# A three-stage float32 kernel: conversion step, weight sums and state-unit loads put in another order

## The chip, the cores and the metric

One core of a Trainium2 chip runs the whole program. The metric is the device time of one execution in microseconds (us), as the median of several runs. All arithmetic is float32; a product is made of three matmuls on pairs of a high and a low part (a value rounded to the matmul's format, and the rest). What the tables call PE is the matmul engine (TensorE), DVE is VectorE, ACT is ScalarE, POOL is GpSimd, and SP is the engine whose queue issues every DMA here.

## The reference

```python
scores = scale * np.matmul(x, state.transpose(0, 1, 3, 2))      # B=8, H=8, S=512, Ns=32, D=64
a = softmax(scores); xread = np.matmul(a, state)
scores2 = scale * np.matmul(state, x.transpose(0, 1, 3, 2))
a2 = softmax(scores2); sread = np.matmul(a2, x)
x = concat([xread, sread]).transpose(0, 2, 1, 3).reshape(4352, 512)
gate = 1.0 / (1.0 + np.exp(-(x @ w_gate))); val = x @ w_val     # w_gate, w_val: 512 x 1536
x = (gate * val) @ w_out                                        # w_out: 1536 x 512
h = x @ w_in; e = np.exp(h - h.max(-1)); solu = h * e / e.sum(-1)   # w_in: 512 x 1024
ln = (solu - mean) / np.sqrt(var + 1e-6) * g_ln
out = ln @ w_out2                                               # w_out2: 1024 x 512
```

The weights arrive as float64. The kernel reads their 32-bit words and builds float32 from them.

## The kernel before

The first two stages go through nine blocks: seven batches, then all state reads together (the block SREAD, 256 tokens wide), then the last batch (in the code `last`, 512 tokens wide). Each block walks c = 0 to 11 over the twelve chunks of 128 hidden columns. In a chunk `first_mm` makes gate and value sums, `sigma` (ACT) and `gated` (DVE) make their product, `gated_hi` (ACT) and `gated_lo` (DVE) split it into `gh` and `gl`, and `out_acc(c-1)` adds the product of the chunk before to four banks `acc`. So the matmul engine works one chunk behind the gate.

For the batches the state is multiplied into the weights ahead of use: a "unit" of 128 x 512 is loaded from DRAM into one of four buffers `spill` (`state_load`, L566 for batches 4 to 7), and `state_w` splits it into `mh` (ACT) and `ml` (DVE). For batches 4 to 7 the units are made by `quad_w` (matmuls L605, copies L610 and L612 into `qst`, DMA L613 to `qsp`) in blocks 2 to 4 and come back from `qsp`, where a unit lies as four pieces of 32 rows.

During SREAD and `last` the weights of the third stage are converted: a `Conv` object loads a tile of words (`load`), takes it apart on ACT (`take`, two ACTIVATEs L207 and L208), forms the float on DVE (`form`, L215, L218, L224), adds the low bits on POOL (`add`, L234) and splits the float into high and low part (`split`). Two buffers hold words (`xn`), two hold floats (`tt`). `step(1)` does this for one tile in each chunk from c = 2. For `w_in` (in SREAD) the split is ACT L134 and POOL L243; for `w_out2` (in `last`) it multiplies by the layer-norm gain as well, ACT L245 (`woh`) and DVE L246 (`wol`). Eight tiles each: taken in c = 2 to 9, split one chunk later.

In `last`, `w_steps` are 24 small steps that make sums and differences of the `w_in` blocks (DVE L739, L742) and split them (ACT L134, DVE L747) into T1 to T4. A table says how many stand in each chunk. After the loop `put` splits the four `acc` banks, and the third stage begins: `h2_mm` for the first tile, its maximum (L788), exponentials, and so on. The first part of that stage is ordered by a scheduler; all before it stands in the order in which it is written, engine by engine, as does the rest of the third stage behind that part.

```python
        def step(self, n):
            for _ in range(len(self.joined)):
                self.split()
            m = min(n, len(self.loaded))
            for _ in range(m):
                self.take()
            self.form(m)
            for _ in range(m):
                self.add()
            for _ in range(n):
                self.load()
```

Of the kernel before, what the change touches and what calls it, by code (L numbers as in the profile page):

```python
# [28 lines left out]
def attn_moe_moe2_kernel(ctx: ExitStack, tc: tile.TileContext, x, state, w_gate, w_val, w_out, w_in2, w_out2, g_ln, out):  # L29
# [4 lines left out]
    nc = tc.nc  # L34
    B, H, S, D = x.shape
    NS = state.shape[2]
# [5 lines left out]
    KC = C // P  # L42
# [36 lines left out]
    spill = [x[:, 512 * i:512 * i + 512] for x in stg for i in range(2)]  # L79
# [42 lines left out]
    qsp = [tc.dram_tile([H, P, 512], F32, name=f"qsp{p}") for p in range(NF1 // 2)]  # L122
# [16 lines left out]
    def lo_of(dst, src, hi):  # L139
        return vec.tensor_tensor(out=dst, in0=src, in1=r(hi), op=ALU.subtract)  # L140
# [17 lines left out]
    class Conv:  # L158
# [87 lines left out]
                vec.scalar_tensor_tensor(out=l, in0=t, scalar=scale, in1=r(h), op0=ALU.mult, op1=ALU.subtract)  # L246

        def step(self, n):
            for _ in range(len(self.joined)):
                self.split()  # L250
            m = min(n, len(self.loaded))
            for _ in range(m):
                self.take()
            self.form(m)
            for _ in range(m):
                self.add()
            for _ in range(n):
                self.load()
# [266 lines left out]
    def ps_acc(m, n):  # L525
        return acc[m][:, 0:n]


    def put(src, h, l, hi=hi_of):
        return hi(h, src), lo_of(l, src, h)  # L530
# [28 lines left out]
    def state_load(b, n):  # L559
        if b < QUAD:  # L560
            nc.sync.dma_start(out=spill[n % 4], in_=msp[b][n])
            return
        p, g = divmod(n, 2)
        r0 = NS * (b - QUAD)
        for k in range(KC):
            nc.sync.dma_start(out=spill[n % 4][NS * k:NS * k + NS], in_=qsp[p][2 * k + g, r0:r0 + NS])  # L566

    def start8(b, p, o, to):

# [97 lines left out]
    def out_acc(c, n, ms=range(KC)):  # L667
        h, l = woh[c], wol[c]
        i = c % 2
        for m in ms:  # L670
            sl = slice(m * P, (m + 1) * P)
            mm3(ps_acc(m, n), h[:, sl], l[:, sl], gh[i][:, 0:n], gl[i][:, 0:n], c == 0, c == NF1 - 1)
# [24 lines left out]
    def yhl(q, k):  # L697
        return yh[q % 2][k], yl[q % 2][k]
# [94 lines left out]
    def h2_mm(i, f, k):  # L793
        q, b, t = tiles[i]
        h, l = yhl(q, k)
        w1, w2 = win(k, f)
        sl = slice(t * P, (t + 1) * P)
        mm3(h2_out(i, f), h[:, sl], l[:, sl], w1, w2, k == 0, k == KC - 1)
# [138 lines left out]
    def loads(n):  # L937

        nonlocal loaded
        loaded = max(loaded, made - M0)  # L940
        while loaded < min(made - M0 + n, len(ring)):
            b, p, g = ring[loaded]
            if b < PAIR and (b, p) in first8 or b < QUAD and early8 and early8[0] <= (b, p) or b >= QUAD and quads and quads[0] <= (p, KC - 1):
                return
            state_load(b, 2 * p + g)
            loaded += 1
# [14 lines left out]
    with tc.manual_schedule():  # L961
# [119 lines left out]
        c = NF1 - 3  # L1081
# [93 lines left out]
        for n_b, b in enumerate(blocks[1:], 1):  # L1175
            before = blocks[n_b - 1]
            n_before = S if before < B else SR
            n = S if b < B else SR
            last = n_b == len(blocks) - 1
            parts = attention(n_b + 1) if n_b + 1 < B else []  # L1180
            if last:
# [18 lines left out]
                w_steps = w_pair_ops([sbf.tile([P, 512], F32, name=f"bf{i}") for i in range(8)])  # L1200
# [5 lines left out]
            for c in range(NF1):  # L1206
# [72 lines left out]
                elif (b == SREAD or last) and c > 1:  # L1279
                    conv.step(1)  # L1280
                if last:
                    for _ in range((3, 3, 1, 2, 1, 2, 1, 2, 1, 2, 3, 2)[c]):
                        w_steps.pop(0)()
        act(stat[0][:, 0:1], half, AF.Exp)
        out_acc(NF1 - 1, S)
        w_steps.pop(0)()
        for k in range(KC):
            ends = put(ps_acc(k, S), *yhl(0, k))
        for k in range(KC):
            for f in range(2):  # L1290
                h2_mm(0, f, k)
# [38 lines left out]
    with tc.manual_schedule():  # L1330
        for i in range(len(first), nt, 2):
            q, b, t = tiles[i]
            n = 3 * ((S if b < B else SR) // P // 2)
# [25 lines left out]
            if i == len(first):  # L1359
                operand()  # L1360
            product(i, 3, w, False, True)
            next_ops(q, ops, step, n)
            plus(w, w, u2)
            h_max(i, 1)
# [71 lines left out]
```

## Time and profile before

| | before |
|---|---|
| median of 3 runs | 1076.2 us (1075.43 to 1076.49) |
| the profiled execution | 1077.1 us, span 1075.3 us |
| PE busy | 1049.0 us, 98% of the span |
| PE weight load busy | 826.8 us, 77% |
| DVE busy | 744.7 us, 69% |
| ACT busy | 569.5 us, 53% |
| POOL busy | 373.5 us, 35% |
| granted PE clock | 0.8 to 0.9 of full in the first slices of 27 us, 0.9 or more after |
| DMA | 148.30 MB, 44.0% of 16 engines on the queue that SP issues on |
| loads of quad state units (L566) | 192 DMAs of 64 KB |

Busy times are sums over the span. The span of the profile is a little shorter than the time of the execution that it belongs to, because starting and ending lie outside it. A row of a timeline gives start and duration of an instruction, its engine and line, the operation, output and inputs, and in brackets how long the engine was idle before it and what it waited for. Instructions of one engine overlap a little, so the distance of two starts can be shorter than the first one's duration.

### The profile page before, as it was taken

Reading aid. Unit: us, or ns where it says so; the run is one execution under the profiler, and the core shown is the slowest. Engines: PE = TensorE matmul, PEld = TensorE weight load, DVE = VectorE, ACT = ScalarE, POOL = GpSimd, SP = SyncE. Lnnn points to the kernel's source line nnn. Section 1 sums busy time; section 2 is a strip of 40 time slices with the busy share of each in tenths; the row PEclk is TensorE's granted clock in tenths of the full one; section 3 lists DMA queues with packets and bytes.
Section 4 is the critical chain, followed back from the end, with each engine's and each line's share of the span. In section 5 each row is a group of like instructions: output and inputs, shape, how many; then the busy total and the mean of one; then the engine's idle time right before and its main releaser. Section 6 shows DMA issues by size and latency. Waiting matters only on the chain.

```text
span 1075.3 us, 16622 instructions
## 1 busy us (share of the span) xinstructions
PE 1049.0 (98%) x5691; PEld 826.8 (77%) x5691; DVE 744.7 (69%) x1323; ACT 569.5 (53%) x1101; POOL 373.5 (35%) x429
## 2 busy tenths in 40 slices
PE   8889999999999999999999999999999999999998
PEld 5555667778877767878878988877888887888887
DVE  5898946658566456565574578968687778777773
ACT  5777645446435434434353455655656555655653
POOL 2687522124000000000000251343767757667551
PEclk8899999999999999999999999999999999999999
DMA  8964183451462662441521434304344444453441
GB/s 221 315 213 162 65 244 121 143 167 38 132 211 102 186 220 84 123 118 46 151 66 50 139 116 156 101 20 157 117 157 155 153 143 138 166 167 121 163 128 39
DMA packets 155740, 148.30 MB, mean 138 GB/s; under 512 B 74888, under 2 KB 115080, under 8 KB 155656
## 3 DMA queue, kind: packets, MB, share of 16 engines
q1 hardware_dynamic: 155656, 147.25, 44.0%
q8 instruction: 44, 0.72, 0.3%
q14 instruction: 40, 0.33, 0.1%
HBM read 91.10 MB, written 56.10 MB: 137 GB/s over the span
## 4 chain that ended last, share of the span: by engine, by line
PE 73%; DVE 9%; DMA 4%; issue 4%; POOL 4%; SPq 3%; ACT 3%; POOLq 0%; DVEq 0%; ACTq 0%
PE acc L143 10%; PE acc L144 9%; PE acc L145 9%; PE att L145 5%; PE att L143 5%; PE att L144 5%; PE gps L143 4%; PE gps L144 4%; PE gps L145 4%; PE vps L143 4%; PE vps L144 4%; PE vps L145 4%; POOL tt L234 1%; PE gps L605 1%; DMA usp<-ub 1%
## 5 line engine op out<-in xcount | busy, mean ns | idle before, releaser
L143 PE MATMUL acc<-gh,woh 128*128 128x512 f32 (+1 forms) x428 | 170.1, 398 | 0.9 <-ACT gh L134 0.9
L144 PE MATMUL acc<-gl,woh 128*128 128x512 f32 (+1 forms) x428 | 162.9, 381 | 1.9 <-DVE gl L665 1.9
L145 PE MATMUL acc<-gh,wol 128*128 128x512 f32 (+1 forms) x428 | 162.7, 380 | 0.0
L234 POOL TENSOR_TENSOR tt<-tt,xn 128x512 int32<-128x512 int32 x16 | 23.5, 1472 | 397.6 <-DVE tt L224 379.4
L659 DVE TENSOR_TENSOR sg<-vps,sg 128x512 f32<-128x512 f32 (+1 forms) x96 | 64.6, 672 | 133.9 <-PE vps L145 97.2
L655 ACT ACTIVATE sg<-gps 128x512 f32<-128x512 f32 (+1 forms) x96 | 55.8, 581 | 141.5 <-PE gps L145 139.3
L143 PEld LDWEIGHTS acc<-gh,woh 128*128 128x128 f32 x428 | 81.0, 189 | 41.1 <-issue 25.1
L134 ACT ACTIVATE gh<-sg 128x512 fp32r<-128x512 f32 (+1 forms) x102 | 61.5, 603 | 74.7 <-DVE sg L659 74.7
L144 PEld LDWEIGHTS acc<-gl,woh 128*128 128x128 f32 x428 | 81.1, 189 | 15.6 <-DVE gl L665 3.0
L145 PEld LDWEIGHTS acc<-gh,wol 128*128 128x128 f32 x428 | 80.9, 189 | 15.7
L870 POOL TENSOR_TENSOR wol<-ut,woh 128x512 fp32r<-128x512 f32 x48 | 61.6, 1299 | 89.7 <-ACT woh L134 87.7
L665 DVE TENSOR_TENSOR gl<-sg,gh 128x512 fp32r<-128x512 f32 (+1 forms) x96 | 66.9, 697 | 19.8 <-ACT gh L134 15.9
L145 PE MATMUL att<-woh,wol 128*128 128x512 f32 (+1 forms) x204 | 79.7, 390 | 0.7 <-POOL wol L870 0.6
L143 PE MATMUL att<-woh,woh 128*128 128x512 f32 (+1 forms) x204 | 79.8, 391 | 0.0
L144 PE MATMUL att<-wol,woh 128*128 128x512 f32 (+1 forms) x204 | 79.3, 389 | 0.0
L143 PE MATMUL gps<-ah,mh 128*128 128x512 f32 x178 | 70.9, 398 | 1.8 <-ACT qst L610 1.1
L144 PE MATMUL gps<-al,mh 128*128 128x512 f32 x178 | 70.1, 394 | 1.2 <-DVE al L140 1.2
L143 PE MATMUL vps<-ah,mh 128*128 128x512 f32 x178 | 69.6, 391 | 0.6 <-DVE ml L140 0.6
L145 PE MATMUL gps<-ah,ml 128*128 128x512 f32 x178 | 69.8, 392 | 0.0
L145 PE MATMUL vps<-ah,ml 128*128 128x512 f32 x178 | 69.4, 390 | 0.0
L144 PE MATMUL vps<-al,mh 128*128 128x512 f32 x178 | 69.3, 390 | 0.0
L544 POOL TENSOR_TENSOR xo<-wf,xe 128x512 fp32r<-128x512 f32 x24 | 32.6, 1364 | 96.6 <-ACT xe L134 91.5
(497 smaller groups left out, 2719.3 us busy)
## 6 DMA issues: line engine op xcount, KB each, us to landing
usp<-ub SPq DMA_DIRECT2D x32, 512.0 KB
ut<-usp SPq DMA_DIRECT2D x128, 128.0 KB
qsp<-qst SPq DMA_DIRECT2D x48, 256.0 KB
stg<-qsp SPq DMA_DIRECT2D x192, 64.0 KB
stg<-msp SPq DMA_DIRECT2D x36, 256.0 KB
out_dram<-sg SPq DMA_DIRECT2D x32, 256.0 KB
xn<-in_x_dram SPq DMA_DIRECT2D x15, 512.0 KB
msp<-pst SPq DMA_DIRECT2D x26, 256.0 KB
```

The source lines that it names most:

```text
L134: return act(dst, src, AF.Copy)
L143: mm(o, lh, rh, start=start, stop=False, **kw)
L144: mm(o, lh, rl, start=False, stop=False, **kw)
L145: return mm(o, ll, rh, start=False, stop=stop, **kw)
L234: pool.tensor_tensor(out=ti, in0=ti, in1=lo, op=ALU.add)
L544: pool.tensor_tensor(out=l, in0=w, in1=r(h), op=ALU.subtract)
L605: mm(o, s[h, k, :], w[h], start=n == 0, stop=n == 2)
L655: act(sg[c % 2][:, 0:n], gate_val(b, c)[0][:, 0:n], AF.Sigmoid)
L659: vec.tensor_tensor(out=g, in0=gate_val(b, c)[1][:, 0:n], in1=g, op=ALU.mult)
L665: eng.tensor_tensor(out=gl[c % 2][:, 0:n], in0=sg[c % 2][:, 0:n], in1=r(gh[c % 2][:, 0:n]), op=ALU.subtract)
L870: pool.tensor_tensor(out=lv, in0=wv[:, 4 * q:4 * q + 4], in1=r(hv), op=ALU.subtract)
```

## The change

Three edits. `step` takes the next tile apart before it splits the last one. The loop over four pieces in `state_load` becomes one DMA whose source is the four pieces as one pattern. The table of `w_steps` ends in 0, 0 in place of 3, 2, and the six steps that are left are issued behind the four `put`s, in the part that the scheduler orders.

```diff
         def step(self, n):
-            for _ in range(len(self.joined)):
-                self.split()
-            m = min(n, len(self.loaded))
+            m, done = min(n, len(self.loaded)), len(self.joined)
             for _ in range(m):
                 self.take()
+            for _ in range(done):
+                self.split()
             self.form(m)
@@ state_load
-        for k in range(KC):
-            nc.sync.dma_start(out=spill[n % 4][NS * k:NS * k + NS], in_=qsp[p][2 * k + g, r0:r0 + NS])
+        nc.sync.dma_start(out=spill[n % 4], in_=qsp[p].rearrange("(k g) r f -> g k r f", g=2)[g][:, r0:r0 + NS])
@@ last
                 if last:
-                    for _ in range((3, 3, 1, 2, 1, 2, 1, 2, 1, 2, 3, 2)[c]):
+                    for _ in range((3, 3, 1, 2, 1, 2, 1, 2, 1, 2, 0, 0)[c]):
                         w_steps.pop(0)()
         act(stat[0][:, 0:1], half, AF.Exp)
         out_acc(NF1 - 1, S)
-        w_steps.pop(0)()
         for k in range(KC):
             ends = put(ps_acc(k, S), *yhl(0, k))
+        for f in w_steps:
+            f()
```

On ACT in SREAD, one chunk. `gh` is the gate's high part, `xe` the high part of a `w_in` tile, `tt` and `xn` are the two results of a take. Before:

```order
L655 ACTIVATE sg_109<-gps 128x256
L134 ACTIVATE gh_95<-sg_109 128x256
L134 ACTIVATE xe_1209<-tt_104 128x512
L207 ACTIVATE tt_103<-xn_99 128x512
L208 ACTIVATE xn_99<-xn_99 128x512
```

The same chunk with the change:

```order
L654 ACTIVATE sg_109<-gps 128x256
L134 ACTIVATE gh_95<-sg_109 128x256
L207 ACTIVATE tt_103<-xn_99 128x512
L208 ACTIVATE xn_99<-xn_99 128x512
L134 ACTIVATE xe_1209<-tt_104 128x512
```

The high part of the last tile has moved behind both instructions of the take.

On ACT in `last`, chunk 4. Before:

```order
L134 ACTIVATE gh_95<-sg_109 128x512
L245 ACTIVATE woh_66<-tt_104,glnt 128x512
L207 ACTIVATE tt_103<-xn_99 128x512
L208 ACTIVATE xn_99<-xn_99 128x512
L134 ACTIVATE T2h_5441<-bf_5471 128x512
```

With the change:

```order
L134 ACTIVATE gh_95<-sg_109 128x512
L207 ACTIVATE tt_103<-xn_99 128x512
L208 ACTIVATE xn_99<-xn_99 128x512
L245 ACTIVATE woh_66<-tt_104,glnt 128x512
L134 ACTIVATE T2h_5315<-bf_5345 128x512
```

`woh` moved in the same way; on DVE the rows of this chunk (gl, `wol`, then L215, L218, L224) stand as they stood.

On DVE, from the gate of chunk 10 to the first maximum of the third stage. Before:

```order
L665 TENSOR_TENSOR gl_97<-sg_109,gh_95 128x512
L246 SCALAR_TENSOR_TENSOR wol_84<-tt_104,glnt,woh_72 128x512
L742 TENSOR_TENSOR bf_5475<-bf_5475,bf_5472 128x512
L747 TENSOR_TENSOR T3l_5448<-bf_5473,T3h_5447 128x512
L739 TENSOR_TENSOR bf_5474<-xe_1214,xo_1215 128x512
L659 TENSOR_TENSOR sg_110<-att_183,sg_110 128x512
L665 TENSOR_TENSOR gl_98<-sg_110,gh_96 128x512
L747 TENSOR_TENSOR T2l_5444<-bf_5475,T2h_5443 128x512
L742 TENSOR_TENSOR bf_5474<-bf_5474,bf_5475 128x512
L747 TENSOR_TENSOR T4l_5452<-bf_5474,T4h_5451 128x512
L140 TENSOR_TENSOR ml<-acc_176,mh 128x512
```

With the change (the lines are one lower behind the shorter `state_load`):

```order
L664 TENSOR_TENSOR gl_97<-sg_109,gh_95 128x512
L246 SCALAR_TENSOR_TENSOR wol_84<-tt_104,glnt,woh_72 128x512
L658 TENSOR_TENSOR sg_110<-att_183,sg_110 128x512
L664 TENSOR_TENSOR gl_98<-sg_110,gh_96 128x512
...
L140 TENSOR_TENSOR wol_85<-acc_179,woh_73 128x512
L741 TENSOR_TENSOR bf_5349<-bf_5349,bf_5346 128x512
L746 TENSOR_TENSOR T3l_5322<-bf_5347,T3h_5321 128x512
L738 TENSOR_TENSOR bf_5348<-xe_1214,xo_1215 128x512
L746 TENSOR_TENSOR T2l_5318<-bf_5349,T2h_5317 128x512
L741 TENSOR_TENSOR bf_5348<-bf_5348,bf_5349 128x512
L746 TENSOR_TENSOR T4l_5326<-bf_5348,T4h_5325 128x512
L787 TENSOR_REDUCE stat_125<-acc_176 128x1
```

Three operations left the place between the two gates, three more the place behind the second, and all six stand behind the four low parts of `put`.

## Rows read from the trace of the kernel before

**Rows 1.** Timeline, one turn of the conversion in SREAD (start us, us, engine, line)
```profile
611.01 1.30 POOL L234 TENSOR_TENSOR tt<-tt,xn 128x512 int32<-128x512 int32 x1 [1.61 <-issue]
...
612.35 0.63 ACT L134 ACTIVATE xe<-tt 128x512 fp32r<-128x512 f32 x1 [0.68 <-POOL tt L234]
...
615.96 1.31 POOL L234 TENSOR_TENSOR tt<-tt,xn 128x512 int32<-128x512 int32 x1 [1.61 <-issue]
```

**Rows 2.** Timeline of PE, start of one group of sums in SREAD
```profile
636.69 0.28 PE L143 MATMUL acc<-gh,woh 128*128 128x256 f32 x1
637.41 0.39 PE L144 MATMUL acc<-gl,woh 128*128 128x256 f32 x1 [0.43 <-DVE gl L665]
637.63 0.28 PE L145 MATMUL acc<-gh,wol 128*128 128x256 f32 x1
637.75 0.28 PE L143 MATMUL acc<-gh,woh 128*128 128x256 f32 x1
```

**Rows 3.** Busy us of PE, PEld, DVE, ACT, POOL (count); clock, DMA share, GB/s
```profile
666.00:703.30 37.30, 37.28 (x165) 30.57 (x164) 36.56 (x55) 22.66 (x40) 11.46 (x7) 1.00 0.35 101
```

**Rows 4.** Timelines of DVE and PE, last two gates of the last row
```profile
704.65 0.69 DVE L665 TENSOR_TENSOR gl<-sg,gh 128x512 fp32r<-128x512 f32 x1 [0.70 <-ACT gh L134]
...
705.94 0.68 DVE L742 TENSOR_TENSOR bf<-bf,bf 128x512 f32<-128x512 f32 x1
...
707.74 0.69 DVE L659 TENSOR_TENSOR sg<-att,sg 128x512 f32<-128x512 f32 x1
...
705.68 0.39 PE L144 MATMUL acc<-gl,woh 128*128 128x512 f32 x1
...
709.20 0.50 PE L143 MATMUL acc<-gh,woh 128*128 128x512 f32 x1 [0.87 <-ACT gh L134]
709.93 0.50 PE L144 MATMUL acc<-gl,woh 128*128 128x512 f32 x1 [0.22 <-DVE gl L665]
```

**Rows 5.** Timelines of the SP queue and PE around 390 us
```profile
379.90 4.97 SPq L566 DMA_DIRECT2D stg<-qsp  x8
...
389.15 1.91 SPq L613 DMA_DIRECT2D qsp<-qst  x4
...
392.05 0.50 PE L143 MATMUL gps<-ah,mh 128*128 128x512 f32 x1 [1.15 <-ACT qst L610]
```

**Rows 6.** Timelines of ACT and DVE, chunks 4 and 5 of the last row
```profile
669.66 0.71 ACT L245 ACTIVATE woh<-tt,glnt 128x512 fp32r<-128x512 f32 x1
670.27 0.65 ACT L207 ACTIVATE tt<-xn 128x512 f32<-128x512 f32 x1
670.83 0.67 ACT L208 ACTIVATE xn<-xn 128x512 int32<-128x512 uint32 x1
...
674.49 0.72 ACT L245 ACTIVATE woh<-tt,glnt 128x512 fp32r<-128x512 f32 x1
...
670.40 0.75 DVE L246 SCALAR_TENSOR_TENSOR wol<-tt,glnt,woh 128x512 fp32r<-128x512 f32 x1
...
675.52 0.74 DVE L246 SCALAR_TENSOR_TENSOR wol<-tt,glnt,woh 128x512 fp32r<-128x512 f32 x1
```

**Rows 7.** Timelines of DVE and PE, two waits in the third stage
```profile
720.54 1.38 DVE L788 TENSOR_REDUCE stat<-acc 128x1 f32<-128x512 f32 x2 [5.68 <-PE acc L145]
...
740.07 0.50 PE L145 MATMUL att<-woh,wol 128*128 128x512 f32 x1 [0.63 <-POOL wol L870]
```

**Rows 8.** SP queue, two state loads; table by stretch, after them and around 390 us
```profile
438.84 1.16 SPq L270 DMA_DIRECT2D xtr<-in_state_dram  x2
...
440.10:441.00 0.90, 0.90 (x5) 0.75 (x4) 0.00 (x0) 0.00 (x0) 0.00 (x0) 1.00 0.21 49
...
390.00:392.50 2.50, 1.35 (x6) 0.81 (x6) 0.36 (x1) 0.60 (x1) 0.00 (x0) 1.00 1.05 393
```

**Rows 9.** Timelines of ACT and PE, a wait for a unit in block 4
```profile
430.66 0.63 ACT L134 ACTIVATE mh<-stg 128x512 fp32r<-128x512 f32 x1 [1.28 <-DMA stg<-qsp]
...
436.93 0.39 PE L144 MATMUL acc<-gl,woh 128*128 128x512 f32 x1
```

## The prediction

> **What bounds the kernel now.** I read the page first (TensorE busy 98% of the span, the clock at 2.4 GHz after the start), then the timeline of each engine around the three edits, then the tables by stretch. Since TensorE is nearly always busy, an edit earns only what TensorE loses by waiting at its place. Such losses are read from the starts of neighbouring matmuls, because the modelled end of one covers part of a gap. Three places matter.
>
> *State read (SREAD block).* A step of the conversion is a loop: the integer add on GpSimd, then the split's high part on ScalarE, then the next take, then three VectorE operations, then the next add. [rows 1] show one turn: the high part starts when the add ends (611.01 + 1.30), the take stands behind it on ScalarE, and the next add 4.95 us after the last. The loop is longer than TensorE's own work for a chunk (36 matmuls of 256 columns at 0.12 us is 4.3 us), so TensorE, which starts ahead, meets it and waits. [rows 2] show such a wait: 0.72 us between two starts where 0.12 is usual, and 0.22 behind it. There are four of these pairs, one in each of the last four chunks that convert a tile.
>
> *Last row.* From 666 to 703.3 us VectorE is busy 36.56 of 37.30 us [rows 3]: it sets the pace, and TensorE's lead shrinks until it waits at the last group of sums [rows 4]. From the start of a low-part matmul of group 10 (705.68) to that of group 11 (709.93) are 4.25 us, where twelve matmuls at 0.2275 us need 2.73: 1.52 us lost.
>
> *Quad state units.* At 390.7 TensorE waits 1.15 us for a ScalarE copy [rows 5], which waits until an earlier write of its buffer has left by a DMA that the SP queue issued only at 389.15, behind eight state loads (4.97 us from 379.90) and eight loads of x.
>
> **The change, part by part.**
>
> *Take ahead of split, state read.* The high part leaves the loop. What is left from one gated product to the next on VectorE is: copy for the high part of the gate, one Abs, the three conversion operations, some 3 to 4 us, under TensorE's 4.3. GpSimd has two operations of 1.3 us a chunk. So the four waits go: 0.60 + 0.10 us each, the first a little less: **-2.7 us**. Everything behind moves up by that, since the last row starts on TensorE's work. Bounds: -2.7 to 0 (the loop closes over GpSimd's subtraction instead).
>
> *Take ahead of split, last row.* Here the low part is on VectorE, and there its place is not changed: it still stands right behind the gate's low part, ahead of the three conversion operations. But on ScalarE its input, the high part, is now behind two more instructions. In an even chunk [rows 6] the high part runs 669.66 to 670.37 and the low part starts at 670.40, with nothing to spare already. Two instructions ahead of it take 0.56 us each as they follow each other (670.27, 670.83): the high part ends at 671.49, the low part starts at 671.52, VectorE stands still for 1.12 us. In an odd chunk the low part starts at 675.52, the high part ended at 675.21, and 1.13 us more give a stall of 0.85. A tile is taken in chunks 2 to 9 and split one chunk later, so in chunks 3 to 9 split and take meet: four stalls of 1.12 and three of 0.85, 7.03, **7.0 us** of VectorE, in a stretch where it had 0.74 us free [rows 3].
>
> What reaches TensorE: the low part of gate 10 ends at 705.34 [rows 4], in the new order 7.0 later, 712.37. TensorE's group 10 had 0.34 us to spare there; now it waits, and its low-part matmul starts at 712.4 (times as if TensorE began the row when it did). Behind it, VectorE has the low part of the weights and then the last gated product at once, since the three w_in sums that stood between (705.94 to 707.74) are gone: product at 705.94 + 7.03 = 712.97. The matmul that needs gate 11's low part started 2.19 us behind the product (709.93 less 707.74): 715.16 at the earliest. TensorE gets there by itself at 712.4 + 2.6 + 0.23, so it no longer waits: 715.25 in place of 709.93. That is 5.3, less 0.1 for the slower next matmul: **+5.2 us**. The earlier groups stay within TensorE's lead or are overtaken by this one. Bounds: -1.5 (VectorE finds cover for the stalls and the wait at 709.20 goes) to +6.
>
> *w_in sums behind the last row.* The 1.8 us saved ahead of gate 11 are in the sum above. The six steps now stand behind the four low parts of the last sums. VectorE was idle 5.68 us there, until TensorE finished the first tile [rows 7]; six operations at 0.6 us are 3.6, about 4.5 with waits for three ScalarE copies: covered, **0**. If the cover were gone each would cost its 0.6.
>
> *Order behind it.* With the six steps in the scheduled part, the scheduler puts one maximum fewer (0.6 us) ahead of the first transpose of that part. That transpose leads, through two DMAs, to the weights for which TensorE waits 0.63 us at 740 [rows 7]. I take **-0.6**; bounds -1.2 to +0.6, since other pieces there change places as well.
>
> *One transfer for four.* 192 issues on the SP queue become 48. Most loads are asked for two chunks ahead, so their issue costs nothing; at 379.90 six fewer at 0.6 us let the write of 389.15 go 3.7 us sooner. But the new source has four groups of 32 rows. The only loads of that form are those of the states, two at 438.84 [rows 8]: the queues carry them at a share of 0.21, some 3.4 of 16 engines, while the writes at 390 ran at 1.05 and 393 GB/s. So a unit of 256 KB takes not 0.67 us of all engines but near 2.7 us of four, and two of them hold these four back by about 4 us more than now: what the queue gives, the engines take. I take **-0.3**, between -1.2 (all engines serve it and the wait of 1.15 goes) and +1.1. The Trainium skill, page "DMA: Bandwidth & Descriptors", section "Rules for kernel authors", says to join many small transfers into one large one; by it this term would be -1.2 and the time 1076.9.
>
> **Sum:** -2.7 + 5.2 - 0.3 - 0.6 = **+1.6 us**. The profiled execution took 1077.1 us (span 1075.3), 0.9 above the median of the runs; it would become 1078.7, and the median 1076.2 becomes **1077.8**. Its own range, from the bounds of the last two terms and one us for the stalls: 1076.0 to 1079.6. A measurement of this kernel can tell some 0.2%, 2.15 us, from no change, so this is no change, near its upper edge.
>
> **The rivals.**
>
> *Faster: the stalls are hidden.* If VectorE had work or time to cover the wait for the high part, only gains are left: -2.7 - 1.5 - 0.3 - 0.6 = -5.1, **1071.1**. For it: the wait at the end of the row is plainly VectorE's doing, and where VectorE is not behind a late input costs it nothing. Against: both queues run in order, and an even chunk has 0.03 us to spare [rows 6]. It decides at the point where the high part ends before the gate's low part does.
>
> *Slower: loads on four engines.* ScalarE already waits 1.28 us for a unit at 430.66 [rows 9], with the copy of a gate behind it. Behind the unit's high part stand that copy and two VectorE operations, some 2 us, so the gate's low part is ready near 432.7, and TensorE takes it up at 436.93: 4.2 us to spare. Two units on four engines (2 x 2.7 us against 2 x 0.67) land 4 us later, and any more is a wait of TensorE. With one us there, and the wait at 390 grown by 1.5 where the forecast has -0.3, it is 2.8 over the forecast: **1080.6**. The point from which it decides is a landing 4.2 us later than now. For it: the share of 0.21. Against: the other units have over ten us of lead. The same page, section "Why a DMA increments its semaphore by 16 and not by 1", says that the number of engines is the largest up to 16 that divides the outermost size on both sides, here four; the trace agrees with its 0.21.
>
> *Slower: the loop closes elsewhere.* GpSimd's subtraction now stands ahead of the next add. If the two and the copy between them make the turn 4.9 us again, the state read gains nothing: 1077.8 + 2.7 = **1080.5**. Against it: two operations of 1.3 us and a copy of 0.6 are 3.2.
>
> **How the numbers follow.** Forecast 0.58, faster 0.14, four engines 0.18, loop 0.10. The range leaves out the faster rival and the low edge: 1075.2 to 1080.8. Slower by over 0.2% (above 1078.35): both slower rivals and about a fifth of the forecast's range, 0.40; faster: its rival, 0.14; the rest 0.46.
>
> **What the changed profile would show.** Right: no low-part wait of TensorE over 0.3 us in the state read; in the last row VectorE idle 0.8 to 1.1 us ahead of seven low parts (wol), put down to ScalarE's woh; TensorE waiting for gate lows or unit lows (ml) from the middle of the row on, the last row some 5 us longer from its first to its last matmul, and less than 2 us of VectorE idle time left ahead of the first maximum. A stretch of state loads alone would run at a DMA share near 0.25. Wrong: wol following gl without idle time; a turn of 4.9 us in the state read; a wait on a state load that TensorE feels.

## The result and the profile after

The change made the kernel **slower: 1090.1 us** (median of 4 runs, 1088.0 to 1091.8) against 1075.8 us (median of 4) for the kernel before, a ratio of 1.0131 (95% interval 1.0113 to 1.015). The prediction was 1077.8 us with a range up to 1080.8: the time lies 9 us above its upper end, and no change that can be measured was its likeliest case. Lines of the changed kernel from L566 on stand one lower than before (the state load is L565, the copies into `qst` L609 and L611, the store to `qsp` L612). By the two profiled executions the difference is 12.8 us.

The page of the changed kernel: its span, busy times (us), and the chain that ended last by engine and by line.

```profile
span 1088.1 us, 16369 instructions
...
PE 1053.9 (97%) x5691; PEld 827.6 (76%) x5691; DVE 745.2 (68%) x1323; ACT 569.3 (52%) x1101; POOL 378.4 (35%) x429
...
PE 70%; DVE 11%; SPq 5%; DMA 4%; issue 4%; ACT 3%; POOL 2%; DVEq 0%; ACTq 0%; POOLq 0%
PE acc L143 9%; PE acc L144 9%; PE acc L145 9%; PE att L145 5%; PE att L143 5%; PE att L144 5%; SPq L299 4%; PE gps L143 4%; PE gps L144 3%; PE vps L143 3%; PE gps L145 3%; PE vps L145 3%; PE vps L144 3%; PE gps L604 1%; DMA qsp<-qst 1%
```

To see is one strange line: the issue of the x loads (SPq L299) has 4% of the chain. Nothing in the edit touches those loads.

TensorE's waits in the changed kernel, longest first (engine, tile and line, releaser: us in total, times, longest):

```profile
PE gps L145 <- DVE ml L140: 4.1, 3, 1.7
PE gps L143 <- ACT qst L609: 3.0, 2, 2.7
...
PE acc L143 <- ACT stg L1341: 1.2, 1, 1.2
...
PE acc L144 <- DVE gl L664: 1.2, 4, 0.6
...
PE att L324 <- DVE ee L349: 1.1, 2, 0.6
```

The first is the last row, the second the place at 390 us [rows 5], the third the third stage, the fourth the state read (0.6 of it in one wait where there were four [rows 2]), the last the x transposes near 470 and 540 us. How long TensorE loses at such a place is read from starts, as in the prediction; a wait in this list can be shorter than that.

To put places in one account I matched TensorE's instructions of two traces in order, by their operands, and took the difference of their start times as a running ledger: the median difference at the end of a stretch, less that at the end of the stretch before. Stretches by the clock of the kernel before; "quad" is where units are stored and loaded back.

| us, less the kernel before | start, to 365 | quad, 365 to 605 | state read, to 645 | last row, to 717 | third stage, to 850 | rest |
|---|---|---|---|---|---|---|
| the change | +0.3 | +6.2 | -1.6 | +5.1 | +2.7 | +0.2 |
| order alone (e1_order) | -0.6 | -0.4 | -2.8 | +6.9 | +0.4 | +0.4 |
| one transfer alone (e2_load) | +2.8 | +8.4 | +3.0 | 0.0 | +0.4 | +0.5 |
| sums alone (e3_sums) | +2.2 | -0.3 | -0.2 | -1.6 | +2.9 | +0.2 |
| all but the transfer (e5_no_load) | -1.5 | -0.4 | -2.8 | +5.1 | +2.9 | -0.2 |
| order in the state read alone (f1_sread) | -1.9 | -0.4 | -2.8 | 0.0 | -0.1 | -0.3 |
| 16-engine transfer (g3_ten) | -1.3 | -2.1 | -0.4 | 0.0 | -0.1 | +0.5 |
| the last two together (b1) | -1.6 | -2.2 | -2.8 | 0.0 | +0.1 | +0.2 |
| x loads first (g1_xfirst) | +0.5 | +10.9 | +3.0 | 0.0 | -0.1 | -0.5 |
| two transfers of 64 rows (g2_two) | -2.2 | +48.4 | +7.9 | +5.7 | +0.4 | 0.0 |
| wol behind the bits (h1_form) | +2.6 | +0.2 | -2.8 | +2.4 | +0.7 | +0.1 |
| b1 and earlier sums (b2) | -1.0 | -2.2 | -2.8 | -0.6 | +0.4 | +0.1 |

The column "start" is no work of any edit (the last section says what it is). The other columns are, to some 0.4 us: in the quad stretch four runs that change nothing there (e1_order, e3_sums, e5_no_load, f1_sread) show -0.3 to -0.4, because TensorE's wait for `qst` [rows 5] is 0.68 to 0.76 us in them and 1.15 in the profiled execution of before. The change's six numbers sum, but for rounding, to 12.8, the difference of the spans. So three places lost: the quad stretch 6.2, the last row 5.1, the third stage 2.7; one gained.

### The profile page after: what moved, and what is told of

The parts are those of the page before. It is cut to its first block, busy times and chain, and to the rows that moved or that the text cites. A ratio compares the mean times of both kernels' runs of the same rounds, so it can differ in the third digit from the quotient of the medians.

```text
span 1088.1 us, 16369 instructions
## 1 busy us (share of the span) xinstructions
PE 1053.9 (97%) x5691; PEld 827.6 (76%) x5691; DVE 745.2 (68%) x1323; ACT 569.3 (52%) x1101; POOL 378.4 (35%) x429
## 4 chain that ended last, share of the span: by engine, by line
PE 70%; DVE 11%; SPq 5%; DMA 4%; issue 4%; ACT 3%; POOL 2%; DVEq 0%; ACTq 0%; POOLq 0%
PE acc L143 9%; PE acc L144 9%; PE acc L145 9%; PE att L145 5%; PE att L143 5%; PE att L144 5%; SPq L299 4%; PE gps L143 4%; PE gps L144 3%; PE vps L143 3%; PE gps L145 3%; PE vps L145 3%; PE vps L144 3%; PE gps L604 1%; DMA qsp<-qst 1%
```

## The experiments

### The parts one by one

**Order alone** (e1_order):

```diff
+            m, done = min(n, len(self.loaded)), len(self.joined)
-            for _ in range(len(self.joined)):
-                self.split()
-            m = min(n, len(self.loaded))
             for _ in range(m):
                 self.take()
+            for _ in range(done):
+                self.split()
```

> The kernel before with the new order of the step alone (takes ahead of the last tile's split), four transfers per state unit and the w_in sums where they were. Theory A (parts add, the sizes are those of the shift between the two traces): the state read gives back 2.7 us, the last row costs about 5 us with its sums still in it, so 1077 to 1079.5 us, with TensorE's waits for gl at L144 gone from the state read and waits for ml and gl new in the last row. Rival B (the order carries the whole loss, the transfers nothing, as the prediction had it for the transfers): 1084 us or more. Rival C (take ahead of split helps, the last row's stall is bought elsewhere): 1074.5 us or less.

Measured: 1081.05 us, before 1077.54 on that chip; ratio 1.004 (1.002 to 1.0059). The time lies above theory A's range, as the kernel before does on this chip; the difference, 3.5 us, fits it. The last row costs 6.9 with its sums in it, not 5. ScalarE and VectorE in the last row of e1_order (start us, us):

```profile
673.53 0.66 ACT L208 ACTIVATE xn<-xn 128x512 int32<-128x512 uint32 x1
674.09 0.71 ACT L245 ACTIVATE woh<-tt,glnt 128x512 fp32r<-128x512 f32 x1
...
681.16 0.65 ACT L208 ACTIVATE xn<-xn 128x512 int32<-128x512 uint32 x1
681.71 0.71 ACT L245 ACTIVATE woh<-tt,glnt 128x512 fp32r<-128x512 f32 x1
...
674.83 0.75 DVE L246 SCALAR_TENSOR_TENSOR wol<-tt,glnt,woh 128x512 fp32r<-128x512 f32 x1 [0.71 <-ACT woh L245]
...
682.45 0.75 DVE L246 SCALAR_TENSOR_TENSOR wol<-tt,glnt,woh 128x512 fp32r<-128x512 f32 x1 [1.02 <-ACT woh L245]
```

`woh` now stands behind the take (L208), and `wol` waits for it, where it waited for nothing [rows 6]. Seven of the eight `wol` of the row wait like this, where none did before: four some 1.0 us and three some 0.7 us, **6.3 us** in all. TensorE meets that as three waits for `ml` (at 673, 687 and 700 us), 4.1 us in all, which it did not have, and some short ones for `gl`.

**One transfer alone** (e2_load):

```diff
-        for k in range(KC):
-            nc.sync.dma_start(out=spill[n % 4][NS * k:NS * k + NS], in_=qsp[p][2 * k + g, r0:r0 + NS])
+        nc.sync.dma_start(out=spill[n % 4], in_=qsp[p].rearrange("(k g) r f -> g k r f", g=2)[g][:, r0:r0 + NS])
```

> The kernel before with one transfer per quad state unit and nothing else. Theory A (a unit occupies few DMA engines for long, and the issues queued behind it on SP are held): +6 to +8 us, 1082 to 1084 us, all of it lost between 375 and 620 us of the span, with x-load issues of 1 to 3 us each where they took 0.49 us. Rival B (the prediction: a saved issue pays for a longer landing): 1074.6 to 1077 us. Rival C (the loss in that stretch came from the moved order in the conversion steps): no x-load issue over 0.7 us, and 1076 us.

Measured: 1090.56 us, ratio 1.0117 (1.0091 to 1.0144): this part alone costs about as much as the whole change. Theory A had the mechanism and too small a size (6 to 8 us; it is 13.0), and the state read lost 3.0 too. In the changed kernel a stretch in which nearly only state units move (table by stretch: busy us of PE, PEld, DVE, ACT, POOL; clock, DMA share, GB/s):

```profile
376.00:377.00 1.00, 0.70 (x5) 0.24 (x3) 0.00 (x0) 0.65 (x2) 0.00 (x0) 1.00 0.26 98
```

A quarter of the 16 DMA engines, at 98 GB/s. At this rate a unit of 256 KB needs 2.7 us, and two behind one another 5.4. What that does is on SP, in the changed kernel, at the place of [rows 5]:

```profile
381.48 1.12 SPq L565 DMA_DIRECT2D stg<-qsp  x2
382.65 8.97 SPq L299 DMA_DIRECT2D e2t<-in_x_dram  x8
391.72 1.91 SPq L612 DMA_DIRECT2D qsp<-qst  x4
```

Issuing two units takes SP 1.12 us instead of 4.97 for eight loads. But the eight x loads behind them take 8.97 us, and so the quad row's store goes at 391.72, not at 389.15. ScalarE's first copy into `qst` there, which needs that store's buffer, in the kernel before and in the changed one:

```profile
391.40 0.60 ACT L610 ACTIVATE qst<-gps 128x512 f32<-128x512 f32 x1 [5.16 <-DMA qsp<-qst]
...
393.92 0.60 ACT L609 ACTIVATE qst<-gps 128x512 f32<-128x512 f32 x1 [5.81 <-DMA qsp<-qst]
```

In both it starts 2.2 us behind the first store's issue. So the transfer itself was not slower here; it was asked for later.

The x loads of the quad stretch by themselves, in the changed kernel (duration in ns: least, median, greatest; first and last start):

```profile
L299 SPq DMA_DIRECT2D e2t<-in_x_dram x48: 449/529/3102, 359.9 to 542.4; - x48
```

Single issues take up to 3.1 us while the units move; in the kernel before the greatest was 1.9, and the eight at this place took 4.14 together. All that stands behind the units on SP is late: x for the transposes at 470 and 540, the store whose buffer TensorE waits for at 390, and the words of `w_in`.

The wait at 390 has a second price. TensorE's matmuls behind it, in the kernel before, the changed one and e2_load (columns as above):

```profile
392.00:398.00 6.00, 5.95 (x32) 3.43 (x33) 4.37 (x7) 2.14 (x4) 0.00 (x0) 1.00 0.86 301
...
394.60:398.00 3.40, 3.40 (x8) 2.73 (x9) 2.69 (x5) 1.52 (x3) 0.00 (x0) 0.50 0.90 301
...
397.00:403.00 6.00, 5.29 (x12) 3.80 (x12) 3.20 (x5) 2.94 (x5) 0.00 (x0) 0.50 0.76 267
```

Behind the wait of 1.15 us the granted clock stayed at 1.00. Behind the waits of 2.73 us (the change) and 2.99 us (e2_load) it was 0.50, the lower level of 1.2 GHz, for 3.4 and 6.8 us, and matmuls started 0.43 us apart, where 0.23 is usual. In the ledger TensorE falls back by another 1.6 and 2.5 us there, of which the transposes behind give back 1.0 and 0.8. The net 0.6 and 1.7 us belong to the one transfer, and their difference is half of that between the two runs' quad stretches, 6.2 and 8.4.

In e2_load ScalarE's first take and the first add of the state read (timelines) wait for the words of `w_in`:

```profile
617.84 0.66 ACT L207 ACTIVATE tt<-xn 128x512 f32<-128x512 f32 x1 [4.32 <-DMA xn<-in_moe_w_in_dram]
...
620.29 1.30 POOL L234 TENSOR_TENSOR tt<-tt,xn 128x512 int32<-128x512 int32 x1 [352.19 <-DVE tt L224]
```

Before, that add ran at 606.06; the ledger puts TensorE 11.2 us later there, so the add is 3 us late beyond that, TensorE's lead over the loop of [rows 1] is gone from the start, and it waits eight times instead of four. With the new order (the change) only one wait is left, which is why the parts do not add in this column: with the one transfer the order is worth 4.6 us, not 2.8.

**Sums alone** (e3_sums):

```diff
-                    for _ in range((3, 3, 1, 2, 1, 2, 1, 2, 1, 2, 3, 2)[c]):
+                    for _ in range((3, 3, 1, 2, 1, 2, 1, 2, 1, 2, 0, 0)[c]):
...
-        w_steps.pop(0)()
         for k in range(KC):
             ends = put(ps_acc(k, S), *yhl(0, k))
+        for f in w_steps:
+            f()
```

> The kernel before with the last six w_in sums behind the last row and nothing else. Theory A (they push VectorE work of the tail back: the shift between the traces grows by about 3.5 us from 720 to 860 us of the span): +1.5 to +3.5 us, with new TensorE waits for woh and stg in the first turns of the tail. Rival B (the prediction: covered by VectorE's idle time ahead of the first maximum, worth 0): 1075.4 to 1076.6 us; the tail's loss then comes from the order or from the later last row. Rival C (VectorE is short in the last row, so fewer sums there help): 1074.5 us.

Measured: 1079.69 us, ratio 1.0017 (1.0 to 1.0035). The median alone can hardly be told from no change, but in the ledger it is two larger things of opposite sign: the row's end gains 1.6 us, the third stage loses 2.9, with the waits that theory A named. VectorE and GpSimd behind the last row of e3_sums:

```profile
714.08 0.68 DVE L742 TENSOR_TENSOR bf<-bf,bf 128x512 f32<-128x512 f32 x1
714.68 1.24 DVE L747 TENSOR_TENSOR T3l<-bf,T3h 128x512 fp32r<-128x512 f32 x1
715.84 1.23 DVE L739 TENSOR_TENSOR bf<-xe,xo 128x512 f32<-128x512 f32 x1
716.99 1.23 DVE L747 TENSOR_TENSOR T2l<-bf,T2h 128x512 fp32r<-128x512 f32 x1
...
721.13 1.27 DVE L788 TENSOR_REDUCE stat<-acc 128x1 f32<-128x512 f32 x2
...
714.35 2.17 POOL L713 TENSOR_TENSOR al<-xtr,ah 128x256 fp32r<-128x256 f32 x2 [9.80 <-ACT ah L134]
716.48 2.34 POOL L713 TENSOR_TENSOR al<-e2t,ah 128x256 fp32r<-128x256 f32 x2
```

The same operation that takes 0.68 us alone takes 1.23 beside GpSimd's subtractions, and these take 2.2 to 2.3 us a pair where the kernel before shows 1.44 (`714.07 1.44` for the same pair). The six operations fill 7.0 us, 0.7 of it a wait, instead of the prediction's 3.6. The idle time of [rows 7] was VectorE's, but not free: GpSimd worked in it. TensorE happens to leave the last row at the same time as in the kernel before (ledger +0.1 in all, a slower start included); the first maximum comes at 721.13, 0.6 us later [rows 7], GpSimd begins its next subtraction at 722.47 in place of 719.68, and TensorE then waits for `stat`, `woh` and `stg`.

**All but the transfer** (e5_no_load), the change with the four state loads put back:

> The change with its one transfer undone (four transfers per quad state unit again); takes ahead of the split and the sums behind the last row stay. Theory A (the parts add: from the traces of the single parts, state read -2.7, last row +7.1 - 2.4, tail +3.7 us): +4 to +6.5 us, 1080 to 1083 us, nothing lost between 370 and 620 us of the span. Rival B (the parts need one another: with the sums gone from the row's end, the order costs nothing): 1075 to 1077 us.

Measured: 1081.62 us, ratio 1.0031 (1.0012 to 1.005). Theory A: its ledger is that of order and sums added (+6.9 - 1.6 in the last row, +5.1 measured), and the quad stretch loses nothing.

### What of the one transfer does the harm

**x loads first** (g1_xfirst): as e2_load, and

```diff
                     y_spill(before, n_before, b)
+                    if n_b > 1 and parts: load_xq(n_b + 1, 1)
                     loads(3)
```

> One transfer per quad state unit (as in the run of that alone, 1090.6 us), and the eight x loads of each row issued ahead of the two state units that stood in front of them on SP. Theory A (the units fill four DMA engines, and SP cannot issue the x loads behind them): the x-load issues fall back to about 0.5 us each, the losses at 390, 470 and 540 us of the span (3.6, 1.8 and 2.0 us) go, and the time is 1082 to 1085 us; what is left is lost where no x load follows a unit (about 615 us). Rival B (the units themselves land too late, whatever stands behind them): 1088 us or more, TensorE's new waits are for mh and ml of the state unit.

Measured: 1091.16 us, ratio 1.0128 (1.0113 to 1.0144): Rival B's size. SP around 390 us, and TensorE:

```profile
381.89 5.46 SPq L299 DMA_DIRECT2D e2t<-in_x_dram  x8
387.40 1.09 SPq L565 DMA_DIRECT2D stg<-qsp  x2
388.59 2.13 SPq L612 DMA_DIRECT2D qsp<-qst  x4
...
397.58 0.80 PE L143 MATMUL gps<-ah,mh 128*128 128x512 f32 x1 [5.33 <-ACT qst L609]
```

The x issues there are shorter again, 5.46 us for eight, as theory A has it, and the store is issued at 388.59, earlier than in the kernel before. Yet TensorE waits 5.33 us for its buffer, longer than in any other run here but the next: the store needs the four engines too, and has the two units, 5.4 us of them, right ahead (from 393 to 397 us the DMA share is 0.24 to 0.27). Near 470 and 540 us it is the units themselves that land late, as Rival B has it; ScalarE in g1_xfirst:

```profile
475.15 0.63 ACT L134 ACTIVATE mh<-stg 128x512 fp32r<-128x512 f32 x1 [5.39 <-DMA stg<-qsp]
```

VectorE's low part and its transposes of x stand behind that. So the harm is not SP's held issue as such: a unit on four engines makes late either what is issued behind it, or what moves behind it, or itself.

**Two transfers of 64 rows** (g2_two):

```diff
-        for k in range(KC):
-            nc.sync.dma_start(out=spill[n % 4][NS * k:NS * k + NS], in_=qsp[p][2 * k + g, r0:r0 + NS])
+        for h in range(2):
+            nc.sync.dma_start(out=spill[n % 4][2 * NS * h:2 * NS * h + 2 * NS], in_=qsp[p].rearrange("(k g) r f -> g k r f", g=2)[g][2 * h:2 * h + 2, r0:r0 + NS])
```

> The kernel before with two transfers of 64 rows per quad state unit in place of four of 32, nothing else. Theory A (a transfer's engines are the groups of rows on its source side, so two transfers of two groups keep two engines busy, 128 packets of 2 KB at 84 ns or 5.4 us for a unit alone and 10.7 us for two behind one another): worse than one transfer, 1094 to 1115 us. Rival B (one big transfer lands late because it is one, so two land sooner): 1080 to 1085 us. Rival C (the two transfers take different engines, four in all): as one transfer, 1089 to 1092 us.

Measured: **1137.75 us**, ratio 1.0566 (1.0547 to 1.0585), beyond even theory A's range: more transfers than in the change, and 47 us slower than it. A stretch of units alone, and two of TensorE's waits:

```profile
422.00:428.00 6.00, 6.00 (x29) 4.71 (x27) 4.08 (x9) 4.84 (x10) 0.00 (x0) 1.00 0.13 51
...
PE att L324 <- DVE ee L349: 10.9, 2, 5.5
PE gps L143 <- ACT qst L610: 10.4, 2, 8.1
```

A share of 0.13 is two engines of 16. The two halves of a unit are issued one right behind the other, so what fits is that both went to the same two engines, but no record names the engine. Either way it is the groups of rows on the source side that count, four or two, not the size of a transfer nor their number.

**One transfer on all engines** (g3_ten): a scratch buffer in which a unit is 128 rows behind one another.

```diff
-        for k in range(KC):
-            nc.sync.dma_start(out=spill[n % 4][NS * k:NS * k + NS], in_=qsp[p][2 * k + g, r0:r0 + NS])
+        nc.sync.dma_start(out=spill[n % 4], in_=qsp[p][4 * g + b - QUAD])
...
-  nc.sync.dma_start(out=qst[r0:r0 + NS].rearrange("n (h d) -> n h d", h=H), in_=state[a].rearrange("h n d -> n h d"))
+  nc.sync.dma_start(out=qst.rearrange("(n a) (h d) -> a n h d", a=4, h=H)[a - QUAD], in_=state[a].rearrange("h n d -> n h d"))
...
-                nc.sync.dma_start(out=qsp[p][2 * k + i], in_=s)
+                nc.sync.dma_start(out=qsp[p].rearrange("(i a) (k n) f -> i k n a f", i=2, n=NS)[i][k], in_=s)
```

> One transfer per quad state unit, but from a scratch buffer whose order makes a unit 128 rows behind one another (the quad states are gathered with their rows interleaved, and the stores of the quad rows write each row to its block's place), so that source and destination both have 128 rows outermost. Same number of stores, 48 loads in place of 192. Theory A (the harm of one transfer was its four engines): no x-load issue over 0.7 us, a unit moved by 16 engines in about 0.7 us, time 1073.5 to 1076.5 us, the wait of 1.15 us for qst at 392 us no longer than before. Rival B (one transfer is harmful by itself, or the scattered store now takes the loss): 1080 us or more.

Measured: 1074.32 us, ratio 0.9975 (0.9961 to 0.9988): faster than before. The quad stretch as a whole (340 to 600 us) and a moment behind two units' issue, g3_ten:

```profile
378.90:379.70 0.80, 0.80 (x6) 0.48 (x6) 0.35 (x1) 0.00 (x0) 0.00 (x0) 1.00 1.03 382
...
340.00:600.00 260.00, 260.00 (x1495) 207.89 (x1494) 146.56 (x261) 107.22 (x201) 0.00 (x0) 1.00 0.42 121
```

and the same 260 us in the changed kernel:

```profile
340.00:600.00 260.00, 255.86 (x1421) 200.84 (x1420) 145.07 (x257) 106.48 (x197) 0.00 (x0) 0.99 0.38 112
```

With 16 engines TensorE does not stand still at all, the 1.15 us of [rows 5] included, and its clock stays at 1.00. Of the -2.1 in the ledger some 0.4 is the scatter named there. One expectation was missed: an x issue still takes up to 1.8 us, as in the kernel before, and costs nothing that can be seen.

### The order: where it helps

**In the state read only** (f1_sread): `step` takes first only if the tile that is to be split has no scale.

> The kernel before with the takes ahead of the split only where the tile has no scale, that is in the state read; the last row keeps its old order, the transfers and the sums are those of before. Theory A: the four waits of the state read (0.6 to 0.7 us each) go and nothing else moves: 1073.2 to 1074 us. Rival B (the state read's gain is given back at the next wait, because the phase of the row is set elsewhere): 1075.5 to 1076.5 us. Rival C (the takes delay the split and TensorE waits for the w_in tiles later): over 1077 us.

Measured: 1074.21 us, ratio 0.9963 (0.9943 to 0.9983); the four waits are gone. A group of sums in f1_sread at the place of [rows 2]: the usual 0.12 us between starts.

```profile
633.08 0.28 PE L143 MATMUL acc<-gh,woh 128*128 128x256 f32 x1
633.20 0.28 PE L144 MATMUL acc<-gl,woh 128*128 128x256 f32 x1
633.32 0.28 PE L145 MATMUL acc<-gh,wol 128*128 128x256 f32 x1
```

**wol behind the bit operations** (h1_form): the order of the change, but in the last row

```diff
+                else:
+                    act(h, t, AF.Copy, scale=scale)
             self.form(m)
+            for t, (h, l), scale in done:
+                if scale is not None:
+                    vec.scalar_tensor_tensor(out=l, in0=t, scalar=scale, in1=r(h), op0=ALU.mult, op1=ALU.subtract)
```

> The kernel before with takes ahead of the split as in the change, but in the last row VectorE's half of the split (wol, L246) stands behind the next tile's bit operations instead of ahead of them; transfers and sums as before. Theory A (the last row's loss in the order alone, 7 us in its trace, is VectorE standing at wol until ScalarE, two takes late, has made woh): most of it goes, and with the state read's 2.7 us gained the time is 1073 to 1075.5 us. Rival B (the loss is not that stall but VectorE's load at the row's end, or woh itself late for TensorE): 1078 us or more, the waits for ml from 690 us on are still there.

Measured: 1077.12 us, ratio 0.9997 (0.9983 to 1.0011). In between: the last row loses 2.4 us where e1_order loses 6.9, and VectorE's idle time from the first to the last `wol` is back at 1.7 us (before 1.5). What remains shows in VectorE's timeline of h1_form:

```profile
690.23 0.75 DVE L262 SCALAR_TENSOR_TENSOR wol<-tt,glnt,woh 128x512 fp32r<-128x512 f32 x1
690.89 1.79 DVE L747 TENSOR_TENSOR bf<-xe,xo 128x512 f32<-128x512 f32 x1
```

In every one of the seven chunks a sum now runs beside GpSimd's integer add at 1.8 us; in the kernel before only four of seven do (1.7 to 1.8), and in three an `ml` at 1.2. Summed, these operations take 12.6 us where they took 10.7: 1.9 of the 2.4. That is the price of this version's own order: in e1_order they take 10.6, as before. So in e1_order the stall of 6.3 us is nearly the whole of the 6.9.

### Versions that beat both

**b1** joins f1_sread and g3_ten; **b2** also does three of the late sums in the row's first two steps, with the table (4, 5, 1, 2, 1, 2, 1, 2, 1, 2, 2, 0).

> The kernel before with takes ahead of the split in the state read only, and one transfer per quad state unit from a scratch buffer in which a unit is 128 rows behind one another. Theory A (the two gains, 2.7 us in the state read and 1.2 us of the wait for qst at 392 us, add): 1071 to 1073.5 us. Rival B (the state read's gain swallows the other, or a wait further on does): 1074 to 1076 us.

> As b1, and three of the w_in sums of the last two steps of the last row done in its first two steps instead, where VectorE is 73 to 96% busy (the rest stay). Theory A (VectorE is short at the end of the last row only; six sums fewer there were worth 2.4 us, three are worth about 1.2): 1070 to 1072.5 us. Rival B (VectorE is short from the first steps on, and the wait only moves): as b1 or up to 1.5 us slower.

Measured: b1 **1073.25 us**, ratio 0.9958 (0.9938 to 0.9977), b2 1073.28, ratio 0.9953 (0.9937 to 0.997), before 1078.12 on that chip. In b1's ledger the gains add, -2.2 and -2.8; by the medians alone neither can be told from f1_sread, whose interval overlaps theirs. b2's earlier sums gain 0.6 in the row and lose 0.4 behind it: Rival B.

## Why the prediction was wrong, point by point

*Take ahead of split, state read*, forecast -2.7: **right**. All runs with the new order show -2.8, but for the change, which has -1.6 because the words of `w_in` are late; the loop did not close elsewhere.

*Take ahead of split, last row*, forecast +5.2 with three sums fewer in it: **right**, +5.1, by the forecast's mechanism. VectorE's stall was put at 7.0 us and is 6.3 (four of 1.0 and three of 0.7 for 1.12 and 0.85; chunks 3 to 9 have only three even ones, but chunk 3 has a long stall too); TensorE loses 6.9 by it, and the sums give 1.6 to 1.8 (forecast 1.8). That the two differences nearly cancel is luck. TensorE meets the stall from the middle of the row on, at three `ml`, and not first at group 10, as the sum had it.

*w_in sums behind the last row*, forecast 0: **wrong, +2.9**. The failed step is the cover: six operations "at 0.6 us are 3.6, about 4.5 with waits", against 5.68 us of idle time [rows 7]. They take 7.0 until the first maximum can start, and they slow GpSimd's splits for the third stage by the same overlap. The trace of before had the price: VectorE's `T1l` takes 1.80 us at 701.55, beside GpSimd's add. The Trainium skill, page "SBUF — State Buffer", section "Who interferes with whom", says that a VectorE instruction with two inputs in that memory contends with a GpSimd instruction that reads from it; the 1.23 us for 0.68 agree, and the statistics L815 with one such input still took 0.69 there (725.75).

*Order behind it*, forecast -0.6: **not seen**. No run has it by itself. In the change TensorE still waits 0.63 us for those weights (at 751.50, as at 740.07 [rows 7]) and 0.76 more just ahead of that.

*One transfer for four*, forecast -0.3, between -1.2 and +1.1: **wrong, and the main miss: +6.2 in the quad stretch and some 1.1 of the state read's gain.** The four engines and 2.7 us a unit were in the text, and are what the runs show. The failed step is "what the queue gives, the engines take": it set 3.7 us of earlier issue against 4 us of later landing, as if the issue did go earlier. It does not: the x loads behind two units are issued more slowly (8.97 us for eight), so the store at 390 goes at 391.72 in place of 389.15, 2.6 us later, not 3.7 sooner. Where it does go sooner (g1_xfirst, by 0.56 us), the engines hold it back and the wait grows by 4.2 us, so the text's "about 4 us" for the landing was right and nothing set it off. The clock at the lower level behind the longer wait, 0.6 us net in the change, was in no sum. And the loss comes at every place where units and other transfers meet, not at 390 alone. The rival of the four engines named the cause and priced it at two places: 390, where the ledger has 2.8 with a first short wait at 377, and 430.66, where it has nothing; x at 470 and 540 us (1.5 and 1.9) and the words of `w_in` at 608 were not on its list. Of the two rules of the Trainium skill's page "DMA: Bandwidth & Descriptors", the one on the number of engines (section "Why a DMA increments its semaphore by 16 and not by 1") agrees with 0.26 for four groups of rows and 0.13 for two. The advice to join small transfers (section "Rules for kernel authors") holds here only where the joined transfer keeps all engines: g3_ten gains 0.25%, e2_load loses 1.2%.

The sum: the forecast's parts are right to a few tenths for the order. Missing are 2.7 us for the sums, the 0.6 of the order behind them, and 7.6 for the transfer (6.2 and 1.1, and the 0.3 that it was to gain).

Left open: what SP's issue waits for in those 3 us (a place in the engines' queues would fit, but no run measured it), the rest of the 2.2 us between the quad stretches of e2_load and the change, and whether GpSimd's later splits or the later maximum makes more of the 2.9 us.

## What to carry to other kernels

Before joining transfers, work out how many engines the joined one keeps (here four groups of rows on the source side kept four, two kept two, 128 rows all 16); if it is fewer, list everything that stands behind it on the queue and on those engines, at each place where it occurs. Idle time of VectorE covers moved work of this kind only if GpSimd is idle there as well. A wait of TensorE can cost more than its length: look at the granted clock behind it. When an instruction is moved ahead on one in-order queue, look at what its follower feeds on the others: the same swap gave 2.8 us where the follower's reader was GpSimd and cost 5 to 7 where it was VectorE, which had 0.74 us to spare in that stretch.

## What the runs showed beyond that

The first 50 us differ from execution to execution by -2.0 to +2.2 us whatever the edit, with TensorE's granted clock. Its mean from 10 to 50 us is 0.96 in the six traces that are 1.6 to 2.0 us ahead of the kernel before, 0.87 in the two that are 0.1 and 0.6 ahead, 0.83 in the kernel before and the change, and 0.79 in the three that are 1.8 to 2.2 behind. From 6 to 22 us in b1 (same columns as above):

```profile
6.00:14.00 8.00, 6.59 (x76) 5.80 (x76) 4.78 (x9) 6.50 (x9) 1.30 (x1) 1.00 1.07 365
14.00:22.00 8.00, 6.06 (x41) 3.53 (x42) 7.24 (x14) 4.96 (x10) 2.35 (x2) 1.00 0.65 126
```

and in e2_load:

```profile
6.00:14.00 8.00, 6.12 (x74) 5.48 (x72) 4.77 (x9) 5.69 (x9) 1.29 (x1) 1.00 1.08 365
14.00:22.00 8.00, 7.02 (x29) 4.34 (x29) 5.88 (x12) 4.12 (x8) 1.30 (x1) 0.54 0.76 150
```

In one the clock stays at 2.4 GHz, in the other it is at the lower level, 1.2 GHz, for most of the 8 us from 14 to 22. Ahead of that TensorE was busy 6.59 of 8 us in the one and 6.12 in the other. That is, for the most part, the column "start" of the ledger, and the reason to read parts of one us from matched traces, not from medians.
